# The first block of a spectral filter feeding an MLP: its last inverse stage on four array quarters, with a DRAM scratch of its own

## The chip, the cores and the metric

The kernel runs on one core of one Trainium2 chip. The metric is the device time of one execution in microseconds. The engines are TensorE (PE; its weight loads are PEld), VectorE (DVE), ScalarE (ACT), GpSimd (POOL) and SyncE (SP). In this kernel SP does nothing but issue DMAs; ScalarE and POOL issue some too.

## The reference

Eight sequences of 3008 tokens and 256 channels are filtered in the frequency domain, and the result goes through a two-layer MLP.

```python
X = np.fft.rfft(x, axis=1)                      # x: (8, 3008, 256)
y = np.fft.irfft(X * (filt_r + 1j * filt_i), n=3008, axis=1).reshape(24064, 256)
h = y @ w_in                                    # (256, 2048), arrives as float64
g = h * np.clip(h + 3.0, 0.0, 6.0) / 6.0
out = g @ w_out                                 # (2048, 256), arrives as float64
```

## The kernel before, in words

**The transform.** 3008 is 64 x 47. A sequence is seen as 47 rows (a) of 64 tokens (c), and both transforms are products with constant tables, in two stages. Because the input is real, only 24 of the 47 frequency residues k are kept (KH = 24). For one sequence the stages are: a transform over a (`a0_unit` and `turn` for sequence 0); `b_unit`, the 64-point stage with its twiddle factors, for two k at a time; `f_unit`, three VectorE products with the filter; `y_unit`, which joins real and imaginary parts; `bi_unit`, the inverse 64-point stage, for four k at a time (unit numbers count pairs of k, so `bi_unit(0, 8)` makes k = 16 to 19); and the last inverse stage over k, which makes 47 tokens for each residue j and its mirror 64 - j. This last stage needs k on the partitions, while `bi_unit` leaves c there. The exchange goes through DRAM: `g_store` writes the scratch `g_tmp` from POOL's queue, and `t4_load` reads it back into the tile `t4`. `n_five` and `n_unit` make the products, and ScalarE copies them into the ring `xn`.

**Even and odd sums.** A token and its mirror have the same cosine part and sine parts of opposite sign. `n_five` makes cosine and sine sums for five residues on four quarters of the array at once (64 partitions by 64 columns each) and keeps the two sums; blocks from the second on use sums and differences in a seven-product scheme of the MLP.

**The first block.** The MLP works on blocks of 512 tokens, 256 pairs. The first block (`plain_up`, `plain_down`) takes its tokens as they are, not as sums. It needs six residues (FIRST = 6 down to 1), which come from sequence 0 as soon as possible:

- k = 0 to 11 come from `g_tmp` by `first_load(0, 12)` (four DMAs on SP's queue).
- k = 12 to 19 come by `first_load(12, 20)` (four DMAs). The stores of k = 12 to 15 are ordinary `g_store`s. Those of k = 16 to 19 are `g0_first(8)`: four small stores of the residues that are needed, two issued by ScalarE and two by SP; the rest of these rows is stored later.
- k = 20 to 23 do not go through DRAM. `direct` multiplies `y` itself, over all 128 partitions, by a table `direct_t` that joins both inverse stages. It opens four accumulators in PSUM (tiles `psn` and `po`).
- `n_first` adds the products of `t4` with the table `edges` into these accumulators, as two strips of 64 columns, and copies them with six ScalarE instructions into `xn`.

**The weights.** They arrive as float64, as pairs of 32-bit words. `w_abs` (ScalarE) and `w_conv`, `w_conv_2` (six VectorE instructions after `w_abs`) make float32 of them, in 16 parts. One part is converted early. `convert(3)` does three more around the first block, and `convert_half`, by a plan of steps, does the others between the steps of the first block. `w_sums` on POOL then makes the weight sums that later blocks need.

**What sets the order.** The order is written out by hand: every engine runs its instructions in the order in which the calls below line 980 make them. A list `plan` says at which step of the MLP which part of the following sequence is made. Each DMA queued by SP or ScalarE takes one of eight completion counters in turn, and waits, before it is issued, until the DMA before it on the same counter has landed. So the eighth DMA before a given one can hold it up.

The calls around the change, before:

```python
convert(j == 4)                       # one conversion, in the first stage
...                                   # b, f, y, bi units and stores
direct(NU - 2); direct(NU - 1)
bi_unit(0, NU - 2, ...)
n_first()
g_store(0, NU - 4); g_store(0, NU - 2)
w_abs(3)
convert(3)                            # then plain_up and plain_down of block 0
```

Of the kernel before, what the change touches and what calls it, by code (L numbers as in the profile page):

```python
# [26 lines left out]
N = 3008  # L27
NA = 47
# [25 lines left out]
PAIRS = BLK // 2  # L54
RING = 3 * PAIRS
ND = (NJ + 1) * TOK
NX = PAIRS - NJ * NA
ATOM = 2 * KH
FIRST = tuple(range(NJ + 1, 0, -1))
# [19 lines left out]
def _make_tables():  # L79
# [62 lines left out]
    def cs_of(x):  # L142
        return np.concatenate([(x[0] + x[1]) / 2, (x[1] - x[0]) / 2])

    def first_of(x, n):
        if n < NJ:
            return np.concatenate(x)
        return np.concatenate([x[0][:NX], x[1][:NX], cs_of([x[0][NX:], x[1][NX:]])])

    rows = np.vectorize(row, excluded=(0, 1))  # L150
    late_rows = np.vectorize(late_row, excluded=(0, 1))
    groups = np.zeros((P, HC, NA))
    ones = np.zeros((P, 2, TOK))
    first = np.zeros((P, NJ + 1, TOK))
    last = np.zeros((P, NJ + 1, TOK))
    direct = np.zeros((P, TC, ND))
    for k in range(KH):
        for j in range(HC):
            for (ri, hh), x in terms(k, j, rows).items():
                if j in FIRST:  # L160
                    first[hh * 64 + ri * 32 + k, FIRST.index(j)] = first_of(x, FIRST.index(j))
                if j < 2:
                    ones[ri * ATOM + hh * KH + k, j] = cs_of(x)
            if j in FIRST:
                for (ri, hh), x in terms(k, j, late_rows).items():
                    last[ri * ATOM + hh * KH + k, FIRST.index(j)] = cs_of(x)
            if j > 1:
                c, s = (terms(k, j, rows)[0, hh][0] for hh in range(2))
                for hh, v in enumerate((c, s)):
                    groups[hh * KH + k, j] = groups[HALF + hh * KH + k, j] = v  # L170
        if k >= KH - TC:
            for q in range(64):
                fr = k + NA * q if q < 32 else NA * (q - 31) - k
                for n, j in enumerate(FIRST):
                    th = [2 * np.pi * ((fr * rows(j, h, a)) % N) / N for h in range(2)]
                    direct[q, k - KH + TC, n * TOK:(n + 1) * TOK] = 2 / N * first_of(np.cos(th), n)
                    direct[HALF + q, k - KH + TC, n * TOK:(n + 1) * TOK] = -2 / N * first_of(np.sin(th), n)
    wai = np.concatenate([t.reshape(P, -1) for t in (groups, ones, first, last)], axis=1)
    f = np.float32
    return wa.astype(f), wai.astype(f), wb.astype(f), wi.astype(f), wf.astype(f), start.astype(f), direct.astype(f)  # L180

# [2 lines left out]
def kernel(  # L184
# [20 lines left out]

    z_d = nc.dram_tensor("z_tmp", (B, KH, 2, HC, 2, D), FP32, kind="Internal").ap()
    g_d = nc.dram_tensor("g_tmp", (B, NC, 2, KH, D), FP32, kind="Internal").ap()

    o_d = nc.dram_tensor("o_tmp", (B * HC * NA, D), FP32, kind="Internal").ap()

# [97 lines left out]
    def w_load(i, q):  # L308
        if W_AT[i] == "g":
            t = gp.tile([P, 7, 256], FP32, name="g")  # L310
            st["rest"] = t[:, 4:7, :].rearrange("p a n -> p (a n)")
            t = t.bitcast(I32)[:, 0:4, :].rearrange("p a n -> p (a n)")
        elif W_AT[i] == "x":
            t = xtp.tile([P, 5, PAIRS], FP32, name="xt").bitcast(I32)[:, 0:4, :].rearrange("p a n -> p (a n)")
        else:
            t = op.tile([P, 1024], I32, name="bits", tag="o")
        q.dma_start(t.rearrange("p (a d) -> p a d", a=2), w_part(i)[0])
        st["bits", i] = t
# [81 lines left out]
    def x0_at(o, n):  # L400
        return w_all.rearrange("p a b c m -> p (a b c m)")[:, ds(NP * 14 * P - HC * D + o, n)]
# [216 lines left out]
        for u in range(2):  # L618
            nc.gpsimd.dma_start(g_d[b, :, :, 2 * (i + 2) + u, :], t[ts(u, 64), 2])

    def g0_first(i):
        t = st["t3", 0, i]
        for v in range(2):
            for h in range(2):
                (nc.scalar, nc.sync)[v].dma_start(g_d[0, ds(h * HC + 1, NJ + 1), :, ds(2 * (i + v), 2), :].rearrange("c ri u d -> c ri (u d)"),
                                    t[ds(v * 64 + h * HC + 1, NJ + 1)].rearrange("p ri u d -> p ri (u d)"))

    def g_store(b, i):
        t = st.pop(("t3", b, i))
        for v in range(2):  # L630
            nc.gpsimd.dma_start(g_d[b, :, :, ds(2 * (i + v), 2), :].rearrange("c ri u d -> c ri (u d)"),
                                t[ts(v, 64)].rearrange("p ri u d -> p ri (u d)"))
# [26 lines left out]
    def first_load(k0, k1):  # L659
        for h in range(2):  # L660
            for ri in range(2):
                p0 = h * 64 + ri * 32
                nc.sync.dma_start(t4[p0 + k0:p0 + k1, 0:NJ + 1, :],
                                  g_d[0, ds(h * HC + 1, NJ + 1), ri, k0:k1, :].rearrange("j k d -> k j d"))

# [54 lines left out]
            ready(i)  # L720


    def direct(i):
        if "psn" not in st:
            st["psn"] = {(c, dh): (psO.tile([P, 2, 2, P], FP32, name="po%d" % (2 + dh)).rearrange("p a u m -> p (a u m)")
                                   if c else psF.tile([P, 512], FP32, name="psn", tag="f"))
                         for c in range(2) for dh in range(2)}
        for u in range(2):
            k = 2 * i + u - KH + TC
            for (c, dh), ps in st["psn"].items():  # L730
                t, n = c * NJ * TOK, (1 if c else NJ) * TOK
                nc.tensor.matmul(ps[:, 0:n], st["y", 0, i][:, u, ts(dh, P)], st["direct"][k][:, ds(t, n)],
                                 start=k == 0, stop=False, skip_group_check=True)

    def n_first():
        for (c, dh), ps in st.pop("psn").items():
            for q, j in enumerate(chunks[c][1]):
                strips(ps[:, ts(q, TOK)], t4[:, j - 1, ts(dh, P)], edges[:, FIRST.index(j), :], start=False, stop=True)
            to = xn[:, dh, :, 0:PAIRS]
            if c == 0:  # L740
                nc.scalar.activation(out=to[:, :, 0:NJ * NA].rearrange("p h (j a) -> p j h a", a=NA),
                                     in_=ps[:, 0:NJ * TOK].rearrange("p (j h a) -> p j h a", j=NJ, h=2), func=AXT.Copy)
                continue
            nc.scalar.activation(out=to[:, :, NJ * NA:], in_=ps[:, 0:2 * NX].rearrange("p (h a) -> p h a", h=2), func=AXT.Copy)
            nc.scalar.activation(out=xn[:, dh, :, ds(PAIRS, NA - NX)],
                                 in_=ps[:, 2 * NX:TOK].rearrange("p (c a) -> p c a", c=2), func=AXT.Copy)

    def xb(k, d, c):
        return xn[:, d, c, ts(k % 3, PAIRS)]
# [13 lines left out]
    def strips(ps, w, x, **kw):  # L763
        for o in range(0, P, STRIP):
            nc.tensor.matmul(ps[ds(o, STRIP)], w[:, ds(o, STRIP)], x, skip_group_check=True, **kw)  # L765
# [214 lines left out]
    with tc.manual_schedule():  # L980
# [23 lines left out]
        def convert(n):  # L1004
            nonlocal done
            for i in range(n):
                w_conv(done)
                w_conv_2(done)
                done += 1
# [27 lines left out]
        for j in range(0, HC, 4):  # L1037
            a0_unit(j)
            convert(j == 4)
        nc.gpsimd.memset(t4, 0.0)  # L1040
        for c in range(FB, NT):
            table_load(0, c)
        last = x0_at(HC * D - 2048, 3 * ND)
        nc.sync.dma_start(last, direct_d[:, 0:3, :].rearrange("p k n -> p (k n)"))
        load_bits(3)
        st["direct"] = [last[:, ts(k, ND)] for k in range(3)] + [st["rest"][:, 0:ND]]
        nc.sync.dma_start(st["direct"][3], direct_d[:, 3, :])
        nc.sync.dma_start(edge, wai_d[:, ds(NW, ND)])
        load_bits(4)
        turn(0)  # L1050
        for c in range(NT):
            for i in (2 * c, 2 * c + 1):
                b_unit(0, i)
                f_unit(0, i)
                if c == NT - 1:
                    y_unit(0, i)
            if c + 1 < NT:
                turn(c + 1)
            if c:
                bi_unit(0, 2 * c - 2)  # L1060
                (g0_first if c == NT - 1 else lambda i: g_store(0, i))(2 * c - 2)
            if c == 4:
                first_load(0, KH - 3 * TC)
        first_load(KH - 3 * TC, KH - TC)
        for i in 1, 2:
            w_abs(i)
        direct(NU - 2)
# [3 lines left out]
        load_bits(6)  # L1071
        nc.sync.dma_start(wa[:, 0:528], wa_d[:, 0:528])
        nc.sync.dma_start(wf, wf_d)
        n_first()
        g_store(0, NU - 4)
        g_store(0, NU - 2)
# [1 line left out]
            x_load(1, c)  # L1078
            load_bits(7 + c)
        w_abs(3)  # L1080
        convert(3)

        def wai_load():
            nc.sync.dma_start(wa[:, 528:], wa_d[:, 528:])
            nc.sync.dma_start(wai, wai_d[:, 0:NW])


        half = 0
# [60 lines left out]
                                 for p in ((2, 3, 6, 7, 12, 13), (4, 5, 10, 11, 14, 15), (11, 16)))  # L1149
            return a_at, f_at, y_at, bi_at  # L1150

        at(n_at[TAIL - 2] + 1, lambda: nc.sync.dma_start(edge, wai_d[:, ds(NW + ND, ND)]))
        at(LAST * NP + 3, b12_back)
        prev = None
        for n in range(1, B):
# [134 lines left out]
```

## Time and profile before

| | |
|---|---|
| time, median of 3 runs | 2609.06 us (2608.47 to 2609.44) |
| span of the profiled execution | 2607.0 us |
| its own time | not recorded apart from the span; the timed runs are 1.5 to 2.4 us above it |
| mean granted TensorE clock | 1.000 |
| busy in 20 to 30 us | PE 8.60, DVE 6.80, ACT 2.79, POOL 0.00 of 10 us |
| busy in 60 to 70 us | PE 8.09, DVE 7.88, ACT 6.52, POOL 2.60 of 10 us |
| busy in 100 to 120 us | PE 20.00, DVE 19.04, ACT 9.69, POOL 4.48 of 20 us |

Times in the profile count from the start of the span. Each matmul of float32 appears as two records of PE, and a group of several gives its whole length. "A <- B" behind an idle time names what ended it. A name such as `psn` or `t` stands for all tiles of that name; `t` is also the name under which `t4` appears. In the chain of work, an entry with DMA is the time from issue to landing, and one with a q (SPq, ACTq) is time of an engine's sequencer.

### The profile page before, as it was taken

How to read it: one execution, taken by the hardware profiler on the slowest of the kernel's cores; microseconds unless marked ns; L12 is line 12 of the kernel's file. 1: busy time of each engine (PE TensorE's matmuls, PEld its weight loads, DVE VectorE, ACT ScalarE, POOL GpSimd, SP SyncE). 2: the span in 40 equal slices, each digit the busy share in tenths (PEclk: the TensorE clock that was granted, in tenths of full speed). 3: DMA queues.
4: the chain of work that ended last, by engine and by line, in shares of the span. 5: the costliest groups of instructions: out<-in, count | busy, mean ns of one | idle time of the engine just before them, and what ended most of it. 6: DMA issues, size and time to landing. Idle time of an engine off the chain costs nothing.

```text
span 2607.0 us, 86613 instructions
## 1 busy us (share of the span) xinstructions
PE 2591.8 (99%) x37708; PEld 2051.0 (79%) x37708; DVE 2053.9 (79%) x3611; ACT 1295.6 (50%) x2677; POOL 486.7 (19%) x711
## 2 busy tenths in 40 slices
PE   8999999999999999999999999999999999999999
PEld 6487777878778787788877888777877778888887
DVE  7978868888788877888778887788877888766666
ACT  4554454545545455444554444545445454455554
POOL 2242021121211202111031210311113120111110
PEclk9999999999999999999999999999999999999999
DMA  8732234112241132411224112331123321110000
GB/s 247 224 92 81 59 101 119 54 33 87 74 123 54 33 87 78 119 54 37 83 83 114 54 38 82 89 108 54 54 66 91 106 57 49 50 44 24 20 22 26
DMA packets 130834, 200.32 MB, mean 77 GB/s; under 512 B 21602, under 2 KB 97472, under 8 KB 130262
## 3 DMA queue, kind: packets, MB, share of 16 engines
q1 hardware_dynamic: 115165, 150.12, 20.4%
q0 software_dynamic: 14720, 44.16, 6.1%
q8 instruction: 296, 4.85, 0.8%
q14 instruction: 84, 0.69, 0.1%
q10 hardware_dynamic: 569, 0.50, 0.1%
HBM read 122.43 MB, written 83.98 MB: 79 GB/s over the span
## 4 chain that ended last, share of the span: by engine, by line
PE 94%; DVE 3%; DMA 2%; POOL 1%; issue 0%; ACT 0%; SPq 0%; POOLq 0%; DVEq 0%; ACTq 0%
PE po L765 43%; PE al L765 24%; PE be L765 18%; PE psn L705 2%; PE psf L540 1%; PE psf L481 1%; PE psf L600 1%; PE be L600 1%; POOL w_all L369 1%; PE be L481 1%; DVE g L818 1%; DMA g_tmp<-t 1%; PE psf L765 0%; DMA ft<-in_filt_i_dram 0%; DVE y L335 0%
## 5 line engine op out<-in xcount | busy, mean ns | idle before, releaser
L765 PEld LDWEIGHTS po<-w_all,g 128*64 128x64 f32 x20808 | 1232.5, 137 | 247.0 <-issue 12.4
L765 PE MATMUL po<-w_all,g 128*64 128x128 f32 (+1 forms) x20808 | 1407.0, 274 | 1.4 <-DVE g L818 0.7
L813 ACT ACTIVATE r<-h,half_c 128x512 f32<-128x512 f32 x736 | 531.0, 722 | 346.7 <-DVE h L794 334.7
L765 PE MATMUL al<-xt,w_all 128*64 128x256 f32 x4416 | 664.0, 379 | 0.4 <-POOL w_all L369 0.3
L818 DVE SCALAR_TENSOR_TENSOR g<-r,h 128x512 f32<-128x512 f32 x736 | 536.2, 730 | 144.6 <-ACT r L813 129.2
L765 PE MATMUL be<-xt,w_all 128*64 128x256 f32 x2944 | 442.6, 379 | 0.0
L794 DVE TENSOR_TENSOR h<-be,s 128x512 f32<-128x512 f32 x368 | 253.8, 690 | 131.3 <-PE be L765 102.2
L760 POOL TENSOR_TENSOR xt<-xn 128x256 f32<-128x256 f32 x184 | 150.7, 838 | 890.3 <-ACT xn L687 890.3
L765 PEld LDWEIGHTS be<-xt,w_all 128*64 128x64 f32 x2944 | 211.3, 137 | 106.5
L765 PEld LDWEIGHTS al<-xt,w_all 128*64 128x64 f32 x4416 | 278.9, 137 | 1.7 <-POOL w_all L369 1.4
L808 ACT ACTIVATE h<-al 128x256 f32<-128x256 f32 x368 | 141.4, 384 | 273.2 <-PE al L765 272.4
L826 DVE TENSOR_TENSOR g<-g 128x512 f32<-128x512 f32 x367 | 261.4, 712 | 12.6
L799 DVE TENSOR_TENSOR h<-al,s 128x256 f32<-128x256 f32 x368 | 156.0, 424 | 135.6 <-PE al L765 130.5
L789 ACT ACTIVATE s<-al 128x256 f32<-128x256 f32 x368 | 141.6, 385 | 207.2 <-PE al L765 207.1
L765 PE MATMUL al<-xn,w_all 128*64 128x256 f32 (+1 forms) x1536 | 240.1, 393 | 1.1 <-DVE g L818 0.7
L765 PE MATMUL be<-xn,w_all 128*64 128x256 f32 (+1 forms) x1536 | 236.4, 388 | 0.0
L780 ACT ACTIVATE s<-be 128x256 f32<-128x256 f32 x368 | 141.4, 384 | 170.1 <-PE be L765 170.1
L825 DVE TENSOR_TENSOR g<-g 128x256 f32<-128x256 f32 x367 | 165.5, 451 | 12.6
L779 ACT ACTIVATE s<-al 128x256 f32<-128x256 f32 x368 | 141.5, 384 | 59.1 <-PE al L765 59.1
L831 DVE TENSOR_TENSOR g<-g 128x256 f32<-128x256 f32 x367 | 161.7, 441 | 2.4
L765 PEld LDWEIGHTS be<-xn,w_all 128*64 128x64 f32 x1536 | 110.3, 137 | 62.3 <-issue 7.4
L506 POOL DMA_DIRECT2D z_tmp<-t x144 | 72.0, 508 | 321.4 <-ACT s L780 296.0
(162 smaller groups left out, 1766.6 us busy)
## 6 DMA issues: line engine op xcount, KB each, us to landing
t<-g_tmp SPq DMA_DIRECT2D x184, 120.0 KB
t<-z_tmp SPq DMA_DIRECT2D x42, 512.0 KB
g_tmp<-t POOLq DMA_DIRECT2D x68, 256.0 KB, 4.3
z_tmp<-t POOLq DMA_DIRECT2D x120, 144.0 KB, 3.7
o_tmp<-o SPq DMA_DIRECT2D x46, 256.0 KB
xs<-in_x_dram SPq DMA_DIRECT2D x60, 192.0 KB
ft<-in_filt_r_dram SPq DMA_DIRECT2D x168, 64.0 KB
ft<-in_filt_i_dram SPq DMA_DIRECT2D x168, 64.0 KB
```

Of the source, the lines that this page charges most:

```text
L760: nc.gpsimd.tensor_tensor(out=o, in0=x0, in1=x1, op=op_)
L765: nc.tensor.matmul(ps[ds(o, STRIP)], w[:, ds(o, STRIP)], x, skip_group_check=True, **kw)
L779: nc.scalar.activation(out=s[:, 0, :], in_=al, func=AXT.Copy)
L780: nc.scalar.activation(out=s5, in_=be[:, 1, :], func=AXT.Copy)
L789: nc.scalar.activation(out=s[:, 1, :], in_=al, func=AXT.Copy)
L794: nc.vector.tensor_tensor(out=st["h"][0].rearrange("p (a n) -> p a n", a=2), in0=be, in1=s, op=ALU.add)
L799: nc.vector.tensor_tensor(out=st["h"][1][:, 256:512], in0=al, in1=s5, op=ALU.add)
L813: nc.scalar.activation(out=r, in_=st["h"][i], func=AXT.Relu, bias=half_c, scale=1.0 / 6.0)
L818: nc.vector.scalar_tensor_tensor(out=st["g", k, p][:, o:o + 2, :].rearrange("p a n -> p (a n)"), in0=st["r", i], scalar=1.0, in1=st["h"][i ...
L825: v.tensor_tensor(out=g[:, G1, :], in0=g[:, G3, :], in1=g[:, G22, :], op=ALU.add)
L826: v.tensor_tensor(out=g[:, G3:G2 + 1:2, :], in0=g[:, G3:G1 + 1, :], in1=g[:, G11:G11 + 1, :].broadcast_to([P, 2, 256]), op=ALU.subtract)
L831: nc.vector.tensor_tensor(out=g[:, G4, :], in0=g[:, G12, :], in1=g[:, G2, :], op=ALU.subtract)
```

## The change

The last stage of the first block is made in even and odd sums on four quarters, as `n_five` does, and so are the direct products; the two are joined on VectorE. With it the tables shrink: `direct_t` has 47 columns for each residue instead of 94, and no table of its own for the first block is left, since the columns of `groups` serve (residue 1 is added to them).

`direct` makes 32 products of 64 x 64 with 282 columns instead of 16 of 128 x 128 with 470 or 94. `n_first` makes 48 products with 47 columns instead of 24 with 94 in two strips; ScalarE copies the even sums (282 columns), VectorE adds and subtracts the odd ones for the 256 pairs of the block, and ScalarE copies the last 26 odd columns.

The late rows, k = 12 to 19, go through a DRAM scratch of their own, `gf_tmp`. `gf_store` writes 38 neighbouring partitions in each of two DMAs, `gf_load` reads six residues in four DMAs per `bi_unit`: for k = 12 to 15 all on SP's queue, for k = 16 to 19 two on SP's and two on POOL's. `g_store(0, 6)` still writes k = 12 to 15 to `g_tmp` for the later blocks. One of the three conversions is moved ahead of `n_first`, the other two stay behind it; on VectorE the four sums of `n_first` stand between the first and the second.

```diff
+NE = (NJ + 1) * NA
...
+    gf_d = nc.dram_tensor("gf_tmp", (2, HC + NJ + 1, 2, TC, D), FP32, kind="Internal").ap()
...
-    def g0_first(i):
+    def gf_store(i, qs):
         t = st["t3", 0, i]
         for v in range(2):
-            for h in range(2):
-                (nc.scalar, nc.sync)[v].dma_start(g_d[0, ds(h * HC + 1, NJ + 1), :, ds(2 * (i + v), 2), :].rearrange("c ri u d -> c ri (u d)"),
-                                    t[ds(v * 64 + h * HC + 1, NJ + 1)].rearrange("p ri u d -> p ri (u d)"))
+            qs[v].dma_start(gf_d[i // 2 % 2, :, :, ds(2 * v, 2), :].rearrange("c ri u d -> c ri (u d)"),
+                            t[ds(v * 64 + 1, HC + NJ + 1)].rearrange("p ri u d -> p ri (u d)"))
+
+    def gf_load(i, qs):
+        for h in range(2):
+            for ri in range(2):
+                qs[h].dma_start(t4[ds(ri * HALF + h * KH + 2 * i, TC), 0:NJ + 1, :],
+                                gf_d[i // 2 % 2, ds(h * HC, NJ + 1), ri, :, :].rearrange("j k d -> k j d"))
...
+    def quarters(ps, dh, w, x, **kw):
+        for g in range(2):
+            for c in range(2):
+                nc.tensor.matmul(ps(c, dh)[ts(g, HALF)], w(c, ds(dh * P + g * HALF, HALF)), x(c), **kw)
...
-            for (c, dh), ps in st["psn"].items():
-                t, n = c * NJ * TOK, (1 if c else NJ) * TOK
-                nc.tensor.matmul(ps[:, 0:n], st["y", 0, i][:, u, ts(dh, P)], st["direct"][k][:, ds(t, n)],
-                                 start=k == 0, stop=False, skip_group_check=True)
+            for dh in range(2):
+                quarters(lambda c, dh: ps[c][dh][:, 0:NE], dh, lambda c, m: y[ts(c, HALF), u, m],
+                         lambda c: st["direct"][ts(c, HALF), ts(k, NE)], start=k == 0, stop=False, skip_group_check=True)
 
     def n_first():
...
+        ps = st.pop("psn")
+        for dh in range(2):
+            for q, j in enumerate(FIRST):
+                quarters(lambda c, dh: ps[c][dh][:, ts(q, NA)], dh, lambda c, m: t4[ds(c * HALF, ATOM), j - 1, m],
+                         lambda c: groups[ds(c * HALF, ATOM), j, :], start=False, stop=True, skip_group_check=True)
+            e, o = (xn[:, dh, c, :] for c in range(2))
+            odd = ps[1][dh]
+            nc.scalar.activation(out=e[:, 0:NE], in_=ps[0][dh][:, 0:NE], func=AXT.Copy)
+            nc.vector.tensor_tensor(out=o[:, 0:PAIRS], in0=e[:, 0:PAIRS], in1=odd[:, 0:PAIRS], op=ALU.add)
+            nc.vector.tensor_tensor(out=e[:, 0:PAIRS], in0=e[:, 0:PAIRS], in1=odd[:, 0:PAIRS], op=ALU.subtract)
+            nc.scalar.activation(out=o[:, PAIRS:NE], in_=odd[:, PAIRS:NE], func=AXT.Copy)
...
-        last = x0_at(HC * D - 2048, 3 * ND)
-        nc.sync.dma_start(last, direct_d[:, 0:3, :].rearrange("p k n -> p (k n)"))
+        st["direct"] = x0_at(HC * D - 2048, TC * NE)
+        nc.sync.dma_start(st["direct"], direct_d.rearrange("p k n -> p (k n)"))
+        nc.sync.dma_start(wai[:, NA:NA + NE], wai_d[:, NA:NA + NE])
         load_bits(3)
-        st["direct"] = [last[:, ts(k, ND)] for k in range(3)] + [st["rest"][:, 0:ND]]
-        nc.sync.dma_start(st["direct"][3], direct_d[:, 3, :])
-        nc.sync.dma_start(edge, wai_d[:, ds(NW, ND)])
...
             if c:
                 bi_unit(0, 2 * c - 2)
-                (g0_first if c == NT - 1 else lambda i: g_store(0, i))(2 * c - 2)
-            if c == 4:
+            if c == NT - 2:
+                gf_store(NU - 6, (nc.sync, nc.sync))
+                g_store(0, NU - 6)
                 first_load(0, KH - 3 * TC)
-        first_load(KH - 3 * TC, KH - TC)
+            elif c == NT - 1:
+                gf_store(NU - 4, (nc.sync, nc.scalar))
+            elif c:
+                g_store(0, 2 * c - 2)
+        gf_load(NU - 6, (nc.sync, nc.sync))
+        gf_load(NU - 4, (nc.sync, nc.gpsimd))
         for i in 1, 2:
             w_abs(i)
         direct(NU - 2)
...
+        convert(1)
         n_first()
         g_store(0, NU - 4)
         g_store(0, NU - 2)
...
         w_abs(3)
-        convert(3)
+        convert(2)
```

## The prediction

> **What bounds the kernel now.** I read the page's busy shares first, then the chain of work that ended last from 40 to 140 us (the edit touches only the start), then VectorE's timeline and the waits of that stretch.
>
> ```profile
> PE 2591.8 (99%) x37708; PEld 2051.0 (79%) x37708; DVE 2053.9 (79%) x3611; ACT 1295.6 (50%) x2677; POOL 486.7 (19%) x711
> ```
>
> TensorE is busy nearly throughout, but this is a mean over stages. The chain (start, length, what) shows the start of the kernel differently:
>
> ```profile
> 50.98 4.56 DMA g_tmp<-t
> 55.56 2.31 DMA g_tmp<-t
> 57.88 0.26 SPq L663
> 58.15 0.04 issue
> 58.19 3.34 DMA t<-g_tmp
> 61.53 0.09 issue
> 61.62 1.86 PE psn L765 x40
> ...
> 67.92 0.70 ACT r L813
> 68.64 0.69 DVE g L818
> 69.33 0.35 DVE y L333
> ```
>
> Frequency rows 16 to 19 (bi_unit 8, called late rows below with 12 to 15) go to DRAM and come back, which takes 10.5 us, with two stores one behind the other. Then come n_first, the first products, and from 67.8 us VectorE, which converts weights until 120.47. There POOL's weight sums start, and TensorE takes over at 139.46:
>
> ```profile
> 119.77 0.70 DVE w_all L361
> ...
> 120.61 0.04 POOL w_all L369
> ...
> 139.46 0.65 PE al L765 x4
> ```
>
> So between 67.8 and 120.5 us the end is set by when VectorE gets through a fixed list. VectorE's timeline and the waits of 50 to 120 us show how little slack it has:
>
> ```profile
> 54.68 0.43 DVE L333 TENSOR_SCALAR y<-bits 128x512 int32<-128x512 int32 x1
> ...
> 58.52 0.42 DVE L333 TENSOR_SCALAR y<-g 128x512 int32<-128x512 int32 x1
> ...
> 65.64 0.69 DVE L354 TENSOR_TENSOR y<-g,y 128x512 f32<-128x512 f32 x1 [1.61 <-ACT g L324]
> ...
> 67.81 0.69 DVE L818 SCALAR_TENSOR_TENSOR g<-r,al 128x512 f32<-128x512 f32 x1
> ```
>
> Conversion 1 runs 54.68 to 58.52, and conversion 2 follows at once: 3.84 us each. They lie under the DRAM round trip. The only VectorE wait listed from 50 to 120 us is the 1.61 in conversion 3, for a ScalarE pass that stands behind n_first's copies. The question is therefore when the second and third conversions end: 67.8 now.
>
> **The change, part by part.**
>
> *Loads.* direct_t drops from 846 + 282 KB to 564, the early piece of wai from 282 to 141: 705 KB less on queues that moved 398 GB/s from 42 to 48 us, so about 1.8 us. The store of rows 8 to 11 landed at 49.78 and let bi_unit's copy start at 49.87; it lands near 48. But that copy reads products that TensorE makes from 48.21 to 50.15, bound by its own order. The two copies end near 50.6 instead of 50.96: 0.35 us of the 1.8 is left.
>
> *Stores.* Four stores of 24 KB become two of 152 KB for rows 16 to 19, and two of 152 KB are added for rows 12 to 15. Gone is the wait of the second SP store for the first ScalarE store (55.56). How long 152 KB takes is not in the trace. Low bound: 2.31 us, the lone 24 KB store, so landing at about 53. High bound: the 4.56 of the row at 50.98, plus the 512 KB of extra store traffic at the 201 GB/s moved from 50 to 52 us, 2.5 us: 57.7. I take 4.8 us, landing at 55.4: its place in the queues, behind first_load's 288 KB, is that of the 4.56 row, and the bi_unit 6 store ahead of it starts a microsecond sooner.
>
> *Loads back.* In the changed instruction order all but one of SP's six late loads, and both on POOL's queue, wait for these stores. On SP five follow each other at 0.44 us (four first_load issues took 1.77), so the last starts 1.8 us after the landing. Landing of such loads took 2.9 to 4.4 us; I take 3.0, as each carries 24 KB instead of 48 or 72. Late rows arrive at 55.4 + 1.8 + 3.0 = 60.2 (bounds 53 + 1.8 + 2.9 = 57.7 and 57.7 + 1.8 + 4.4 = 63.9), against 61.53. POOL's pair has 0.6 us per issue and 3.7 to 4.3 to land: 59.7 to 60.3, with three stores of g_tmp queued behind it whose readers come at 74 us.
>
> [...]
>
> *Direct products.* Before: 16 products on the full array, 8 of 470 columns and 8 of 94, from 51.16 to about 59.6. After: 32 products of 282 columns on quarters. Two 470-column products took 1.61 us (53.56 to 55.17), 1.7 ns a column, so 0.48 us each; four at a time 3.9 us, one at a time 15.4. The nearest row is n_five's (L705, same quarters): 40 products of 47 columns in 1.31 us, 33 ns each instead of 80, at least 2.4 at a time, hence at most 6.4 us. The half that needs y_unit's end at 54.65 takes 1.9 to 3.2, bi_unit 10 another 1.1: TensorE is free at 57.7 to 59.0, under the 60.2. Cost nothing; without that cover (one at a time) n_first would start at 63.5, 3.3 late.
>
> *n_first.* 24 products of 47 columns per half at 33 ns, 0.79 us. ScalarE's copy of 282 columns is about 0.41 (256 took 0.384, 470 took 0.57). VectorE's sums of 128x256 from PSUM are 0.42 each (L799, 425 ns). In order after arrival: products ready and copy started +1.1, copied +1.5, two sums +2.4, the 26-column copy (0.2 as L744 and L745 took; it waits for the difference) and the second copy +3.1, two sums +4.0. Before, the matmuls took 2.2 us and six ScalarE copies 2.0; now 1.6 against 2.9 of copies and sums. [...]
>
> *The order on VectorE.* Conversion 1 stays ahead of n_first, the four sums come next, conversions 2 and 3 behind them. This is the new wait: from 58.5 VectorE stands still until the first sum at 60.2 + 1.5 = 61.7, with every later conversion queued behind it. Conversions 2 and 3 then end at arrival + 4.0 + 2 x 3.84 = arrival + 11.7 = 71.9, against 67.8. The 1.61 wait goes (ScalarE's pass is done before conversion 3 needs it) and is counted in this. TensorE starts the first block about 1.6 us sooner (62.6, was 64.22), but its results wait for VectorE.
>
> *Sum.* +4.1 us on VectorE at 67.8, nothing to absorb it up to 120.5, passed to POOL and TensorE. The span was 2607.0, the timed runs 2608.47 to 2609.44, so about 2.1 lies around it. 2609.06 + 4.1 = 2613.2. Bounds of arrival: 57.7 gives +1.6, 63.9 gives +7.8. A gain needs arrival before 56.1. About 0.2%, 5.2 us, is what a measurement of this kernel can tell from no change, so the forecast lies inside that: slower, but hardly to be seen.
>
> **The rivals.**
>
> *Stores land late.* The added 512 KB delays them in the queues. Decides from arrival 61.3 on (stores at 56.5); priced at the high bound, +7.8, 2616.9: slower. For it: queues were 0.7 to 0.86 busy from 50 to 54 us. Against: only 0.10 from 54 to 56.
>
> *The delay is taken up.* TensorE, 51.35 of 52.7 us busy in this stretch, sets the end, and starts 1.6 us sooner: 2607.5 to 2609. Against: it waits for VectorE's g, and POOL waits 15.9 us for the last conversion.
>
> *The quarters do not overlap.* Start of n_first at 63.5, +7.4, 2616.5. Against: L705.
>
> *A gain over 5.2 us* needs arrival at 50.9, before the copies of those rows have ended (50.96). Only something outside this chain could bring it.
>
> **How the numbers follow.** Forecast 0.51, taken up 0.12 (both within 0.2%), late stores 0.30, no overlap 0.03 (slower), gain 0.04. Faster 0.04, same 0.63, slower 0.33. The range runs from the taken-up case to the late bound: 2608 to 2617.
>
> **What would show it.** VectorE idle from 58.5 to about 61.7, then four sums of 0.42; the first L818 at about 71.9; its last conversion before POOL's sums near 124.6 instead of 120.47; TensorE's late-row products at 60.2; the direct products twice as fast. Wrong if the late rows arrive before 57 or after 64, or if the last conversion moves without the end moving with it.

## The result, and the profile after

The changed kernel took 2629.49 us (median of 4 runs, 2627.96 to 2630.36) against 2608.76 us for the kernel before (4 runs, 2607.78 to 2609.44). The ratio is 1.0082, 95% interval 1.0070 to 1.0094: 20.7 us slower, where 4.1 were forecast, and above the range (2608 to 2617). The profiled execution took 2630.36 us, its span is 2628.6, 21.6 more than before.

The chain of work that ended last, of the changed kernel (start, length, what):

```profile
48.50 0.84 SPq L617
...
49.38 14.09 DMA gf_tmp<-t
...
63.83 4.04 DMA t<-gf_tmp
...
68.12 0.53 POOL t L623
68.65 0.09 issue
68.74 5.99 DMA t<-gf_tmp
...
86.74 0.61 DVE g L821
87.35 0.04 issue
87.39 3.68 PE al L768 x8
91.07 2.96 PE be L768 x8
```

The store in this chain is the second of the two for rows 12 to 15. It is in flight for 14.09 us. The two stores for rows 16 to 19, which the forecast priced at 4.8 us, take 11.76 (ScalarE's, issued at 51.84) and 12.70 (SP's, issued at 54.66, landing at 67.36) by the trace's record of the completion counters. The last rows come back at 74.73 us, not 60.2. The row at 87.39 is one that the prediction did not look for: the same eight records of `al` took 1.94 us before. TensorE's timeline of the kernel before:

```profile
68.55 1.94 PE L765 MATMUL al<-xn,w_all 128*64 128x512 f32 x8 [0.68 <-DVE g L818]
70.32 1.89 PE L765 MATMUL be<-xn,w_all 128*64 128x512 f32 x8
```

SP's queue (start, length, line, how many) in the same stretch, and POOL's loads; the first row is `first_load` in the kernel before, the others are the changed kernel's:

```profile
49.91 1.77 SPq L663 DMA_DIRECT2D t<-g_tmp  x4
...
48.50 1.53 SPq L617 DMA_DIRECT2D gf_tmp<-t  x2
50.48 4.08 SPq L661 DMA_DIRECT2D t<-g_tmp  x4
54.66 0.97 SPq L617 DMA_DIRECT2D gf_tmp<-t  x1
63.54 1.29 SPq L623 DMA_DIRECT2D t<-gf_tmp  x4
67.42 0.59 SPq L623 DMA_DIRECT2D t<-gf_tmp  x2
...
68.12 1.22 POOL L623 DMA_DIRECT2D t<-gf_tmp  x2 [18.23 <-DMA t<-gf_tmp]
```

The four issues of `first_load` (L661) take 4.08 us instead of 1.77, so the last store leaves SP late and lands at 67.36. The loads wait for it: SP issues the four for rows 12 to 15 at 0.33 us each, stands still, and issues its two for rows 16 to 19 at 67.42. POOL's pair goes out at 68.12, 0.76 us after that landing. (The chain puts POOL's start down to a load that landed at 67.88. In p39, a run below, POOL's pair also goes out 0.76 us after the last store, and there that load lands only afterwards.)

VectorE's timeline (in brackets the idle time before, and what ended it):

```profile
58.92 0.69 DVE L354 SCALAR_TENSOR_TENSOR w_all<-s,y 128x512 f32<-128x512 f32 x1
76.77 0.42 DVE L747 TENSOR_TENSOR xn<-xn,po 128x256 f32<-128x256 f32 x1 [17.16 <-ACT xn L746]
...
78.72 0.42 DVE L748 TENSOR_TENSOR xn<-xn,po 128x256 f32<-128x256 f32 x1
79.06 0.42 DVE L326 TENSOR_SCALAR y<-g 128x512 int32<-128x512 int32 x1
...
86.66 0.68 DVE L821 SCALAR_TENSOR_TENSOR g<-r,al 128x512 f32<-128x512 f32 x1
```

This is the wait the prediction described, at five times its length: VectorE stands still after conversion 1, makes four sums of 0.42, two conversions, and reaches the first hard swish (L821, L818 before) 11.93 us after the rows arrived; 11.7 were forecast.

Busy time by stretch, with the granted TensorE clock (PEclk) after the engines:

```profile
58.00:62.70 4.70, 0.69 (x7) 0.00 (x0) 1.54 (x3) 0.00 (x0) 0.00 (x0) 1.00 0.13 44
62.70:79.80 17.10, 5.22 (x102) 3.74 (x104) 2.31 (x6) 2.31 (x7) 3.59 (x6) 0.50 0.68 220
79.80:86.60 6.80, 2.62 (x12) 0.63 (x8) 6.42 (x11) 3.49 (x6) 0.00 (x0) 1.00 0.62 144
86.60:93.40 6.80, 6.01 (x14) 1.71 (x16) 6.49 (x13) 1.91 (x3) 0.00 (x0) 0.50 0.24 78
```

TensorE has nothing to do while it waits for the rows, and again while VectorE converts; each time its clock falls to 0.50. The first drop slows `n_first`, ahead of VectorE's list: from the last row to the first sum it takes 2.04 us, against 1.43 in warm2 (below), where the clock is at 1.00 there. The second, 86.6 to 93.4, meets the products that come straight after the first hard swish, and these are on the path: 3.68 + 2.96 instead of 1.94 + 1.72 us.

So the span splits in three: rows 13.2 us later (74.73 against 61.53); 5.7 us more between the rows and the first hard swish (11.93 against 6.28); and 2.7 us behind it. Of the last, 3.0 is the halved clock, and 0.3 is given back.

### The profile page after: what moved, and what is told of

Same layout as the page of the kernel before. It is cut to its first block, busy times and chain, and to the rows that moved or that the text cites. A ratio compares the mean times of both kernels' runs of the same rounds, so it can differ in the third digit from the quotient of the medians.

```text
span 2628.6 us, 86793 instructions
## 1 busy us (share of the span) xinstructions
PE 2592.8 (99%) x37788; PEld 2052.2 (78%) x37788; DVE 2055.0 (78%) x3615; ACT 1293.9 (49%) x2675; POOL 487.2 (19%) x713
## 4 chain that ended last, share of the span: by engine, by line
PE 96%; DMA 2%; DVE 1%; issue 0%; ACT 0%; SPq 0%; POOL 0%; POOLq 0%; DVEq 0%; ACTq 0%
PE po L768 44%; PE al L768 25%; PE be L768 18%; PE psn L703 2%; PE psf L533 1%; PE psf L474 1%; PE psf L593 1%; PE be L593 1%; PE be L474 1%; DMA gf_tmp<-t 1%; DMA t<-gf_tmp 0%; DMA ft<-in_filt_i_dram 0%; PE psf L768 0%; DMA wa<-wb_t 0%; PE psf L447 0%; DMA w_all<-in_x_dram 0%
## 5 line engine op out<-in xcount | busy, mean ns | idle before, releaser
L821 DVE SCALAR_TENSOR_TENSOR g<-r,h 128x512 f32<-128x512 f32 x736 | 535.1, 729 | 144.9 <-ACT r L816 129.8
L768 PEld LDWEIGHTS be<-xn,w_all 128*64 128x64 f32 x1536 | 110.9, 137 | 63.4 <-issue 9.0
```

Of the source, the lines that this page charges most:

```text
L821: nc.vector.scalar_tensor_tensor(out=st["g", k, p][:, o:o + 2, :].rearrange("p a n -> p (a n)"), in0=st["r", i], scalar=1.0, in1=st["h"][i ...
```

## The experiments

The changed kernel makes one theory of three parts: (A) a store of 38 partitions uses only two of the 16 DMA engines; (B) the order on VectorE adds its own delay; (C) the halved clock adds 2 to 3 us. The rival to A is the one of the prediction: the added bytes fill the engines' queues, however they are spread.

All runs together. "First sum" is the start of the first L747 (where VectorE waits for the rows, the last one lands 2.0 to 2.2 us before it if the first half of `n_first` runs at half clock, 1.4 to 1.6 if at full clock, as in warm2 and p39_sp); "swish" is the start of the first hard swish; "rest" is the span minus that; the last column is the median minus the median of the kernel before on the same chip.

| kernel | first sum | swish | rest | median - before (us) |
|---|---|---|---|---|
| before | - | 67.81 | 2539.2 | 0 |
| after | 76.77 | 86.66 | 2541.9 | +20.7 |
| before_gf | - | 84.05 | 2539.2 | +17.9 |
| p39 | 68.61 | 78.49 | 2542.3 | +11.1 |
| p41 | 90.38 | 100.26 | 2540.6 | +35.1 |
| old_path | 61.84 | 71.72 | 2540.0 | +5.9 |
| p39_sp | 64.40 | 74.28 | 2542.3 | +11.9 |
| p39_order | 66.96 | 76.85 | 2542.5 | +14.4 |
| conv2 | 68.64 | 74.85 | 2539.9 | +7.2 |
| warm | 83.49 | 93.37 | 2539.0 | +26.5 |
| warm2 | 77.79 | 87.67 | 2539.9 | +19.1 |
| old_conv | 63.53 | 69.75 | 2539.4 | +2.5 |
| mended | 65.47 | 71.67 | 2539.4 | +5.1 |
| best | - | 75.38 | 2539.5 | +8.6 |
| one_unit | 64.01 | 70.23 | 2538.7 | +2.8 |
| old_warm | 62.02 | 68.27 | 2538.7 | +2.0 |

Two columns carry most of what follows. From the first sum to the swish it is 9.88 or 9.89 us in every kernel with the order of the change, and 6.20 to 6.25 in every kernel with two conversions ahead. And the rest is 2538.7 to 2539.9 us wherever the products behind the swish run at full clock (`al` and `be` there take 3.7 us together), and 2541.9 to 2542.5 in four of the six kernels where they do not: after, p39, p39_sp and p39_order, with 5.3 to 6.6 us. The other two are old_path (5.0 us, rest 2540.0) and p41 (5.3 us, rest 2540.6). So the length of these two groups does not fix the rest by itself: p39 and p41 have the same 5.3 us and rests 1.7 apart. Whatever delays the first hard swish comes out at the end in full.

Each row is one execution, and the executions are apart before the change has any part in it: ScalarE's copy of rows 16 to 19, ahead of the late stores, ends at 50.96 us before, 51.82 after, 51.01 in mended, 53.42 in best, 53.56 in warm2 and 50.37 in old_warm. The copies of that kind some 19 us earlier are spread as widely (31.73 to 34.90). Differences of up to 3 us in the first two columns can be no more than this; the last column has medians.

**p39 and p41: one partition more, three more** (A against the bytes)

```diff
-    gf_d = nc.dram_tensor("gf_tmp", (2, HC + NJ + 1, 2, TC, D), ...)
+    gf_d = nc.dram_tensor("gf_tmp", (2, 39, 2, TC, D), ...)          # p41: 41
-    t[ds(v * 64 + 1, HC + NJ + 1)]
+    t[ds(v * 64 + 1, 39)]                                            # p41: 41
```

> The changed kernel with gf_store writing 39 partitions instead of 38 (one more row that nobody reads, 2.6% more bytes). Theory A (spread): a store of 38 partitions is worked off by very few DMA engines. The profile of the changed kernel shows it: 76 packets of 0.084 us each went out over 7.2 us with about one in flight, and four such stores together took from 48.5 to 63.5 us. 38 is 2 x 19, 39 is 3 x 13. If the spread follows the divisors, 13 engines share the store: it lands in 3 to 5 us instead of 14.1, the late rows arrive at about 60 us instead of 74.73, TensorE does not fall to half clock, and the time is 2612 to 2615 us. [...] Theory B (bytes): three times the bytes in the queues are what takes the time, then nothing changes: 2629 to 2631 us.

> The changed kernel with 41 partitions in gf_store, 8% more bytes. 41 has no divisor but 1. Theory A: one engine takes all four stores, 328 packets of 0.084 us, 27.6 us instead of the 12.8 of 304 packets on two engines; the late rows arrive some 14 us later than in the changed kernel, 2642 to 2647 us. Theory B (bytes): about 1 us more than the changed kernel, 2630 to 2632 us.

Measured: p39 2619.39 us (2618.32 to 2622.57), ratio 1.0040 [1.0025, 1.0055]; p41 2643.40 us (2642.68 to 2644.11), ratio 1.0130 [1.0115, 1.0145]. p41 is where theory A put it. p39 is faster, as A has it, but by less: 2612 to 2615 us and rows at about 60 were expected, and the rows come at 66.55. Set against the kernel before on the same chip, more bytes make the changed kernel 9.6 us faster at 39 partitions and 14.4 us slower at 41. The chain and SP's queue of p41:

```profile
49.64 23.81 DMA gf_tmp<-t
```

```profile
51.85 15.05 SPq L661 DMA_DIRECT2D t<-g_tmp  x4
67.01 0.64 SPq L617 DMA_DIRECT2D gf_tmp<-t  x1
```

In the trace's packet records a store is cut into packets of 2048 bytes that take 84 ns at the median. In the changed kernel the four stores have about 2.0 of them in flight in nearly every microsecond from 52 to 61 us: 4 x 76 packets x 84 ns / 2 = 12.8 us for the four, two at a time and with nothing else between. In p41 it is 1.0, in p39 mostly 3.6 to 8. The record of the completion counters says it directly. After an update at the issue, the counter of a store goes up twice more for 38 partitions, once for 41 and 13 times for 39; there are 16 updates for the 48 of mended, and six after the first for the small stores of six partitions in the kernel before. Read as one update for each engine that takes part, which is the author's reading, 38 partitions go to two. Each of these counts (2, 1, 13, 16 and 6) divides its number of partitions (38, 41, 39, 48 and 6); what it is for other numbers, these stores don't show. The bytes as the cause are refuted for the main part.

What is issued behind the stores stands in line with them, as far as the counters tell. The first DMA of `first_load` has 12 updates behind the one at its issue: in the changed kernel ten have come by 54.23, and the last two at 62.54 and 63.67 (the second store lands at 63.47); in p41 eleven have come by 65.14, the last at 73.71 (the second store at 73.45). The issue on SP gets longer as well, from 1.77 us (before) to 4.08 (two engines) to 15.05 (one). That isn't the narrow spread alone, though: it is 4.63 in p39 and 5.63 in mended, with 13 and 16 engines by the counters.

**before_gf: the scratch alone, in the kernel before**

```diff
-                (g0_first if c == NT - 1 else lambda i: g_store(0, i))(2 * c - 2)
...
+                gf_store(NU - 6, (nc.sync, nc.sync)); g_store(0, NU - 6); first_load(0, KH - 3 * TC)
...
+        gf_load(NU - 6, (nc.sync, nc.sync)); gf_load(NU - 4, (nc.sync, nc.gpsimd))
```

> The other part alone: the kernel before the change, with the late rows through the scratch of its own (38 partitions, loads as in the changed kernel). The late rows should arrive at about 74.7 us as in the changed kernel. The three conversions are then done long before, so the first product of the MLP starts at about 77.4 and VectorE's first g at about 80 to 82 (half clock included), 12 to 14 us after before's 67.8: 2621 to 2624 us by theory A and by theory B alike; if the arrival is earlier than 70 us, the slow arrival belongs to the quarters and not to the scratch, and the time is under 2618.

Measured: 2626.16 us (2624.98 to 2626.78), ratio 1.0065 [1.0048, 1.0082]; above what was expected. The rows arrive at 76.1, later than in the changed kernel: SP's store of rows 16 to 19 has the completion counter of ScalarE's, and goes out at 61.93, when that one has landed (11.16 and 6.50 us in the chain); and n_first, coming after a wait of 15.68 us, takes 3.40 us for `psn` instead of 1.85, which the expectation had not counted. The scratch alone makes most of the loss, 17.9 of 20.7 us (the two parts are not quite a sum: the 17.9 here and the 5.9 of old_path, below, are 3.1 us more than both together). The clock does not fall behind the swish there (`al` 1.94): in the order of the kernel before, TensorE's only wait between n_first and these products is one of 0.66 us, where the changed kernel has 4.98.

**old_path, old_conv, conv2: the order on VectorE** (B)

```diff
 # old_path: the rows of the changed kernel go the old way
-                gf_store(NU - 6, (nc.sync, nc.sync))
-                gf_store(NU - 4, (nc.sync, nc.scalar))
+                g0_first(NU - 4)
-        gf_load(NU - 6, ...); gf_load(NU - 4, ...)
+        first_load(KH - 3 * TC, KH - TC)
 # old_conv = old_path with, conv2 = p39_order (below) with
-        convert(1)
+        convert(2)
         n_first()
...
-        convert(2)
+        convert(1)
```

> One part alone: the quarters, the even and odd sums and the new order of the conversions stay, but the late rows go through g_tmp as before the change (four small stores of six partitions, loads of eight k at once). If the scratch is the whole loss beyond my forecast, the late rows arrive at about 61.5 us, conversions 2 and 3 end 11.7 to 11.9 us later at 73.3, 5.5 us after before's 67.8, and the time is 2613 to 2616 us. If the products on quarters or the sums are themselves the loss, it stays above 2622 us. If a delay on VectorE there is taken up later, it is 2608 to 2611 us.

> The late rows go the old way (through g_tmp) as in old_path, and two conversions instead of one stand ahead of n_first, one behind it. Rows at 60.3, conversions 1 and 2 done by 62.4, four sums 62.4 to 64.1, conversion 3 until about 68: first hswish within half a microsecond of the kernel before, no idle stretch that halves the clock, 2608.5 to 2610.5. If VectorE's order is not what old_path's 5.5 us were (the sums or the quarters themselves cost), it stays at 2613 to 2614.

> As p39_order, with two conversions ahead of n_first on VectorE and one behind it, instead of one and two. My account says that VectorE stands still from 58.5 us to the first sum and that conversions 2 and 3 behind the sums cost the 4 us of the forecast. With conversion 2 in that gap the sums begin at about 62.4 us, conversion 3 ends at 68 to 68.5 us (67.8 before the change), and the time is 2608 to 2610 us. If VectorE's order is not what costs, the time stays with p39_order at 2612 to 2614.

Measured: old_path 2614.13 us (2613.46 to 2614.77), ratio 1.0021 [1.0011, 1.0030]; old_conv 2611.03 us (2609.56 to 2612.08), ratio 1.0010 [1.0001, 1.0018]; conv2 2614.74 us (2612.43 to 2616.43), ratio 1.0026 [1.0016, 1.0037], against 2621.97 for the same kernel with one conversion ahead. old_path is where its first case put it (2613 to 2616). With the rows at their old time the change still costs 5.9 us, of which moving one conversion gives back 3.4. old_conv stays 0.5 us above its range, and two things expected of it did not come: its first hard swish is 1.9 us behind that of the kernel before, not within 0.5, and the clock falls. In conv2 the level was missed (2608 to 2610 was expected, its rows came late, at 66.4) but the step is larger, 7.2 us between the medians: 3.7 by the order and 2.6 in the rest, where the second drop of the clock is gone (`al` 1.94 instead of 3.68); the 0.9 left over is not accounted for.

The line of old_conv's first products, in TensorE's timeline, shows what takes the place of VectorE's list there:

```profile
64.55 3.68 PE L774 MATMUL al<-xn,w_all 128*64 128x512 f32 x8 [3.49 <-DVE xn L754]
67.99 2.43 PE L774 MATMUL be<-xn,w_all 128*64 128x512 f32 x8
```

Before, the direct products and n_first kept TensorE busy up to 63.8 us but for waits of at most 1.0 us. On quarters the same work is done by 61 us, TensorE waits 3.5 us for the sums, the clock is at 0.50 from 62.2 to 69 us, and `al` and `be` end 2.2 us later than they would. Faster products have bought a slower clock.

**warm, warm2, old_warm: keep TensorE busy while it waits** (C)

```diff
+    def idle(ps, n):
+        for i in range(n):
+            nc.tensor.matmul(ps[:, 0:256], st["start"][:, 0:P], st["start"][:, 0:2 * P], start=True, stop=True)
...
+        idle(psO.tile(..., name="po0"), 32)      # warm: 36 into psU "al"; old_warm: 7, behind n_first
         n_first()
...
+        if p == 0:                               # warm and warm2, in plain_up
+            idle(psO.tile(...), 12)
```

> The changed kernel with TensorE kept busy while it waits: 36 products of 256 columns that nobody reads before n_first, and 12 after the first two products of the MLP. In the changed kernel the granted clock is 0.50 from 62.7 to 79.8 and from 86.6 to 93.4 us; the products that release VectorE's work from 87.4 us take 3.68 and 2.96 us instead of 1.72 each, and n_first's first half 1.5 instead of 0.8. If the idle time makes the clock fall, it stays at 1.00 here, and the time falls by 3 to 4 us, to 2625 to 2627. If the lower clock has another cause or costs nothing on the way to the end, the time stays at 2629 to 2630.

> The changed kernel with 32 products of 256 columns, whose results nothing reads, ahead of n_first in a bank that nothing holds, and 12 more behind the first half's MLP products. The rows still arrive at about 74.7 us. If the rest that the arrival and the list on VectorE leave over is the halved TensorE clock, the products after the first hswish take 1.9 and 1.7 us again instead of 3.7 and 3.0, and the time falls by 2.5 to 3.5 us, to 2626 to 2627. If the halved clock is hidden by VectorE's list, the time stays at 2629 to 2630.

> old_conv with 7 products of 256 columns, read by nothing, behind n_first, where TensorE stood idle from about 61 to 64.5 us. If the halved clock after that idle time is what old_conv still loses, al and be take 1.9 and 1.7 us instead of 3.7 and 2.2, the second hswish comes 0.7 to 2.5 us sooner, and the time is 2608.5 to 2610.3. If VectorE's list alone sets the end there, it stays at 2610.5 to 2611.5.

Measured: warm 2634.06 us (2631.97 to 2635.05), ratio 1.0099 [1.0082, 1.0116]; warm2 2627.63 us (2626.84 to 2629.42), ratio 1.0075 [1.0062, 1.0089]; old_warm 2610.02 us (2608.72 to 2610.77), ratio 1.0007 [0.9998, 1.0016].

warm missed its aim: its products write the tile `al`, which a copy of ScalarE (64.01 to 64.62) still had to read; that copy waited for the late store, which landed at 63.91, so the products began at 64.66 and held n_first back until 82.1. Its rest of 2539.0 still shows what a full clock is worth: 2.9 us against the changed kernel. warm2 writes a tile that is free (`po0`), and its second products run at full speed (its median is 0.6 us above what was expected):

```profile
84.09 5.45 PE L723 MATMUL po<-p 128*128 128x256 f32 x24
89.47 1.94 PE L772 MATMUL al<-xn,w_all 128*64 128x512 f32 x8
91.23 1.89 PE L772 MATMUL be<-xn,w_all 128*64 128x512 f32 x8
```

From the first hard swish to the end of `be` it is 5.5 us (87.67 to 93.1) instead of 7.4 (86.66 to 94.03): 1.9 less, and 1.1 of the gain is lost again because the idle products themselves end only at 89.47, after VectorE is done. The times of the two profiled executions agree: 2629.42 with the swish 1.0 later, against 2630.36. So C holds by the traces, at 1.9 us gained and about 3.0 in all; the medians, 1.6 us apart over before, have overlapping intervals and would not show it alone. In old_warm the clock is at 1.00 for these products (`al` 2.25), but against old_conv only 0.5 us is gained (2.0 instead of 2.5 over before), too little to be told apart with intervals of this width; there VectorE's list is as long (6.25 us from the first sum to the swish, 6.22 in old_conv).

The stretches at 0.50 are 17.1 and 6.8 us long in the changed kernel, 6.8 in old_conv and 3.4 in old_path, within 0.1 us five, two, two and one times 3.4. The waits that go with them have no one length. In old_conv the clock falls at 62.23, 1.2 us into the wait of 3.49. In old_path it falls at 54.73, and the only wait of TensorE in the 3 us before is one of 1.44 us; the same 1.44 us left it at 1.00 in the changed kernel. The stretch in old_path, busy throughout (engines, then the clock):

```profile
54.80:58.10 3.30, 3.30 (x32) 1.85 (x28) 3.06 (x6) 1.60 (x3) 0.00 (x0) 0.50 0.36 77
```

So a wait of 1.44 us can be enough, and when it is, these runs don't show.

**p39_sp, p39_order, one_unit: what holds the rows once the stores are spread**

```diff
 # p39_sp = p39 with
-        gf_load(NU - 4, (nc.sync, nc.gpsimd))
+        gf_load(NU - 4, (nc.sync, nc.sync))
 # p39_order = p39_sp with first_load(0, KH - 3 * TC) behind the last late store
 # one_unit = mended (below) with rows 12 to 15 through g_tmp
-                gf_store(NU - 6, (nc.sync, nc.sync))
-        gf_load(NU - 6, (nc.sync, nc.sync))
+        first_load(KH - 3 * TC, KH - 2 * TC)
```

> The kernel with 39 partitions, and the two late loads of POOL's queue issued by SP instead. With 39 partitions the stores no longer take 14 us, yet the late rows still arrive at 66.55 us and not at 60: POOL's two loads are issued at 60.11 and 60.73 and the last takes 5.82 us for 24 KB, while the weights of 512 KB each that SP queues after its own loads pass on the same DMA engines. If it is that place in the queues, the loads on SP go ahead of the weights, arrive at about 63.5 us, and the time falls by 3 us, to 2615 to 2617. If a load of 24 KB from four k-rows is slow by itself, nothing changes: 2618 to 2621.

> As p39_sp, and in addition SP issues first_load(0, 12) after the last late store instead of before it. With 39 partitions SP needs 4.63 us to issue the four first_load DMAs (1.77 before the change), and the store behind them goes out at 56.05 us, 4 us after its data are there. If this queueing is what is left of the late arrival, the store goes out at about 51, the late rows arrive at 59 to 60 us, and the time is 2612 to 2614, where my forecast put the changed kernel. If the arrival is set by the DMA engines and not by SP's order, it stays with p39_sp.

> The mended kernel with only rows 16 to 19 through the scratch; rows 12 to 15 go through g_tmp as in the kernel before, so two of the four large late stores are gone. If those two stores are what lengthens first_load's issue and holds the last store: first_load's four issues take 1.8 us again instead of 5.6, rows arrive near 60 to 61, and the time is 2610 to 2612. If the four-row loads or the spread of the store itself hold the rows, first_load's issue still comes down but the rows stay at 62 to 64 and the time at 2613 to 2614.

Measured: p39_sp 2619.50 us (2617.03 to 2621.01), ratio 1.0044 [1.0029, 1.0059]; p39_order 2621.97 us (2619.50 to 2622.25), ratio 1.0052 [1.0037, 1.0067]; one_unit 2610.84 us (2609.68 to 2613.66), ratio 1.0012 [1.0003, 1.0021].

In both of the first two the gain that was expected did not come. Moving POOL's pair to SP brings the rows 4 us sooner in the profiled execution, but the medians over before are the same (+11.1 and +11.9), so it isn't shown that the pair costs anything. Putting `first_load` behind the late stores is no help either: the last late loads have the completion counters of its DMAs and wait until these land (6.74 us in flight, to 60.87, in p39_order's chain). one_unit takes away two of the four stores, those ahead of `first_load`, and there the issue of `first_load` is short again:

```profile
50.47 1.96 SPq L661 DMA_DIRECT2D t<-g_tmp  x4
52.54 0.72 SPq L617 DMA_DIRECT2D gf_tmp<-t  x1
```

That part of the expectation came in (1.96 against 5.63 in mended), and so did the time, 2.3 us lower than mended's. The rows are at 62.6 us, as the other case had it, but they no longer decide alone: conversion 2 ends at 63.93, ScalarE's copy of `n_first` at 63.99, and the first sum follows at 64.01. The intervals of the two kernels overlap, so the 2.3 us are likely rather than shown; whether they would be the stores' bytes or their place in SP's queue, no run separates. Either way it is the rival's part, at about a tenth of the loss.

**mended and best: versions with the faults out**

```diff
 # mended = the changed kernel with 48 for HC + NJ + 1 in gf_d and gf_store, all of gf_load on nc.sync,
 # and convert(2) ahead of n_first, convert(1) behind
 # best = before_gf with 48, all of gf_load on nc.sync, first_load(0, KH - 3 * TC) behind the last late store
```

> The whole change with 48 partitions per late store (16 queues instead of 2), POOL's two late loads on SP, and two conversions ahead of n_first. If the stores' spread and VectorE's order are the whole loss: rows at 62 to 64, first hswish at 70 to 72, 2610 to 2613. If first_load and the added store bytes hold the rows as in p39_order (65 to 67): 2613 to 2616. Neither theory expects it under the kernel before.

> The kernel before with the scratch alone: 48 partitions per late store, first_load issued behind the last late store, all late loads on SP; direct products, n_first and VectorE's order as before. Rows arrive at 62 to 65 instead of 61.5, and every microsecond past 61.5 passes to the end: 2609 to 2612. A scratch whose stores spread over all queues that still costs 5 us or more would mean that the store bytes, not the spread, carry the cost.

Measured: mended 2613.58 us (2612.67 to 2617.21), ratio 1.0023 [1.0014, 1.0031]; best 2617.14 us (2616.64 to 2618.56), ratio 1.0035 [1.0022, 1.0049]. mended gives back 15.6 of the 20.7 us; its rows come at 63.4 and its rest is that of before, as the case of spread and order had it, but its time lies in the other case's range. It has the order of old_conv and differs in the scratch, on the same chip: 2.6 us between the medians is what the scratch costs there with its stores on 16 engines by the counters. best is 5 us above what was expected, and over the 5 us that it was to take as a sign for the bytes. But more than the spread is in it. Its rows come at 67.5, 4.1 us behind mended's. Its copy of rows 16 to 19 ends 2.4 us after mended's, which the spread of the executions may account for. And `first_load`, put ahead of the late loads, holds them: its last DMA waits until 59.65 for the counter of ScalarE's store, and the loads leave SP from 60.07 to 62.74 us. n_first then runs at half clock (3.08 us for `psn` instead of 1.85). How much of the 8.6 us is left for the bytes, the runs don't settle. No version beats the kernel before, and none of the runs points to one that would.

## Why the prediction was wrong

The mechanism was seen, and its first link mis-sized.

*Stores: the step that failed.* The prediction priced a store of 152 KB between a lone 24 KB store and the rate of all queues together, and took 4.8 us, at most 57.7 us for the landing of rows 16 to 19. It counted bytes and never asked over how many engines these bytes go. By the counters, 38 = 2 x 19 partitions go to two, and the small stores, of 6 partitions, to six. Measured: 12.70 us, landing at 67.36 instead of 55.4. Of these 12.0 us, 7.9 are the flight, 2.8 the wait for `first_load`'s issues on SP, which the working did not count, and 1.2 the copies, which ended at 51.82 and not at 50.6 (no more than executions differ there). Both bounds were rows of other, wider spread traffic, so no range made from them could hold this.

*Loads back.* 1.8 + 3.0 us were forecast after the landing, 7.4 measured (67.36 to 74.73). SP's last two loads landed by 70.03, no slower than forecast; POOL's pair decides. It goes out 0.76 us after the landing, its second load 0.62 later, and that one landed after 5.99 us, not 3.7 to 4.3. This is the second mis-sized term. Together the rows came 14.5 us later than forecast.

*Loads less, direct products.* They decide nothing, as forecast for the products: these run four at a time, each record 0.40 to 0.45 us, and TensorE is free at 58.7, inside the 57.7 to 59.0 of the working and 16 us before the rows.

*VectorE's order.* Right: arrival + 11.7 forecast, 11.93 measured, and from the first sum to the swish all eight kernels with this order agree to 0.01 us. That the total fits so well is partly luck: the first sum came 2.04 us after the rows instead of 1.5, by the half clock, and the sums and conversions took 9.9 instead of 10.2. old_path, where the rows are on time, is the forecast's own case: +4.1 forecast, +5.9 measured, of which its trace shows 3.9 at the swish and 0.8 in the rest.

*Nothing absorbs it.* Right: the rest moves by 1.3 us over the kernels with a rest of up to 2540.0, while the swish moves by 26. The rival of a delay taken up is refuted. POOL's sums begin at 141.77 instead of 120.61.

*The clock: missing from the sum.* That TensorE would wait was in the working: for the rows, and from its first products, which start at 62.6, until VectorE's list ends at 71.9. What the waits do to its clock was not. Of the 21.6 us it makes the 2.7 behind the swish and about 0.5 ahead of the first sum; in old_path it is 0.8 behind the swish at most, which is hardly outside the spread of the rests at full clock.

*The rivals.* Late stores was the case that came, decided from the arrival it named (61.3), but for another reason than the 512 KB and at 20.7 us instead of 7.8. The quarters do overlap. A gain had no chance.

## What to carry to other kernels

Before pricing a small DMA by its bytes, factor the number of partitions that it spans: 38 and 41 against 39 made 10 and 24 us here, and what was issued behind the stores paid too (the first DMA of `first_load` was complete only at 63.67, and at 73.71 with 41). When a reorder puts a wait in front of a list on one engine, price the list from the wait's end, and look at what the waiting does to TensorE: the idle stretch ahead of the first hard swish was paid a second time here, with 3.0 us in the products that follow it on the path. And to see where a delay goes, subtract: the time from one fixed event to the end tells in one number whether anything later has changed.

## What had not been expected of the hardware

- One partition more or less changes a store: the second of the late stores is 14.09 us in flight with 38 partitions, 23.81 with 41, but 6.06 with 39 (p39) and 6.72 with 48 (mended); the first, with no other late store ahead, 7.83, 15.19, 4.61 and 4.59.
- An issue can take long by itself: four DMAs of `first_load` took SP 1.77 us before and 1.96 in one_unit, with no late store ahead, and 4.08 with two on two engines, 15.05 with two on one, but also 4.63 and 5.63 with two on 13 and 16. What sets the length is open.
- A speed-up of products can lower the clock: in old_conv TensorE finished its direct products and n_first 3.5 us early, its clock stood at 0.50 from 62.2 to 69 us, and it paid 2.2 us for that.
- A wait of 1.44 us ahead of busy TensorE was followed by 3.4 us at half clock in old_path, and by none in the changed kernel.
